# Block-sparse attention into a hard-swish MLP: k, q and x turned by the DMA crossbar instead of TensorE and VectorE

## The chip, the cores and the metric

The kernel runs on one core of one Trainium2 chip. The metric is the time of one execution in microseconds (us); the times shown are those of three executions, and one more execution was recorded by the hardware profiler. Engines are called PE (TensorE), ScalarE (ACT), VectorE (DVE), POOL (GpSimd) and SP (SyncE, which here only issues DMAs).

## The reference

q, k and v have 4 batches, 8 heads, 768 rows and 64 columns in float32. Each row attends to its neighbours at a distance below 16 and to 24 block summaries (the maximum of k and the mean of v over blocks of 32 rows). The output of all heads, 3072 x 512, goes through two matrix products with a hard-swish between them.

```python
k_sum = k.reshape(B, H, nb, block, D).max(axis=3)
v_sum = v.reshape(B, H, nb, block, D).mean(axis=3)
scores_l = scale * np.matmul(q, k.transpose(0, 1, 3, 2))
mask_l = np.abs(pos[:, None] - pos[None, :]) < window
scores_s = scale * np.einsum('bhsd,bhnd->bhsn', q, k_sum)
scores_s = scores_s + np.log(block)
scores_l_m = np.where(mask_l, scores_l, -1000000000.0)
scores_all = np.concatenate([scores_l_m, scores_s], axis=-1)
...
v_all = np.concatenate([v, v_sum], axis=2)
...
x = np.ascontiguousarray(attn_out.transpose(0, 2, 1, 3)).reshape(B * S, H * D)
...
h = x @ w_in
relu6 = np.clip(h + 3.0, 0.0, 6.0)
g = h * relu6 / 6.0
return (g @ w_out).astype(np.float32)
```

## The kernel before

Queries are handled in 12 tiles of 64 per batch and head. A tile t sees 96 keys: 32 rows ahead of its own window start, then 64 rows, and 24 block summaries, 120 in all. `kaug[p]` holds them for head pair p with the head columns on the partitions: [128, 12 tiles, 128], columns 0 to 31 the rows ahead, 32 to 95 the tile's own rows, 96 to 119 the block maxima. `vaug[i]` (two buffers, batch b uses b % 2) holds v with keys on the partitions, rows 0 to 31 being the rows ahead, 96 to 119 the block sums. q is shifted by 16 rows against k and lies turned in `qT`. Half 0 of a batch is tiles 6 to 11, half 1 tiles 0 to 5.

The steps, by the tags that they carry in the order text (tag, batch, index):

- **K, Q, V, I, O, Q01w**: loads by POOL, with a cast to bf16: k, q, v, w_in in four parts, w_out in four parts, and the rows of q for batch 0's half 1 (`qwide`). Batch 0's k and q come in their own layout (`knat`, `qnat`). Batch 1 comes in rows (`load_nat`, `nat`), batches 2 and 3 in blocks of 32 columns (`load_raw`, 32x96x32 pieces, `kraw` and `qraw`).
- **k0p, q0p**: batch 0's k and q turned by PE transposes, copied out of PSUM; `q_rest` (q0p1) turns q of half 1 from `qwide` on PE.
- **w1p** (`turn_nat`): per head pair, six PE transposes of k and six of q, copies out of PSUM, the copy of the rows ahead (`third`) and the block maxima (`maxima`). **w2p, w3p** (`turn`): the same for batches 2 and 3, but k and q turned by VectorE in 32x32 blocks.
- **h0cx**: the rows ahead of v in batch 0, copied by ScalarE or VectorE (`halo`); **H1 to H3** (`halos`): the same for batches 1 to 3 by two DMAs within SBUF, issued by SP.
- **u** (`vsum`): block sums of v on PE, then copies into `vaug`.
- **s** (`scores`): 12 small matmuls per half, exponential on ScalarE, mask on VectorE. **v** (`values`, `finish`): values, normalisation into `xn`, and xn turned into `x`: by PE and a copy for batches 0 and 1, by a crossbar DMA on SP (line 745) for batches 2 and 3.
- **F** (`f1`): first MLP product of a tile of 384 tokens (line 771), r on ScalarE (776), g on VectorE (778). **G** (`f2`): second product (791), copy, store by SP (802, 803). Eight token tiles s = 2 * batch + half.

What runs in which order on each engine is written out by hand: the `ORDER` text lists every step as tag.number, with :A or :D for the engine where ScalarE and VectorE are both possible. A small planner (`Plan.run`) walks the text, gives out the PSUM banks and buffers, and reckons a start for each step from costs that stand in the code; the program is issued in the order of these starts, and each engine takes its own instructions in that order. `keep` puts idle matmuls on PE into gaps that the planner reckons ahead of 23 us. Line 479 is the helper by which all copies go, line 876 the idle matmuls. SP and POOL also take their DMAs in order, and at most eight DMAs are open on each side (a ninth waits for the first).

Of the kernel before, what the change touches and what calls it, by code (L numbers as in the profile page):

```python
# [29 lines left out]
K01.0 K02.0 c.0 z2.0 z0.0 e.2 e.3 c.8 z3.0 z1.0 Q000.0 K00.0 c.2 Q010.0 c.4 e.1 V00.0 c.1 k02.0 k01.0 k02.1 e.0 s030.0 k03.0  # L30
k02.3:A k03.2:A q010.0 k02.2:A q010.1:A q000.0 q000.1:A q020.0 k01.1 k03.1 k03.3:D k03.4 k00.0 q030.0 q030.1:A s030.1 s030.2
V01.0 V02.0 V03.0 c.6 Q01w1.0 Q01w0.0 I0.0 Q01w2.0 c.7 k00.1 k00.3:D q020.1:D h010.0:A k01.4 s010.0 u00.0 u00.1:A k01.2:A
h000.0:A u01.0 s000.0 s010.1 h011.0:D k00.2:D k00.4 u02.0 s000.1 k01.3:D s010.2 u00.2:A s000.2 u03.0 h020.0:D u01.1:D u01.2:D
h030.0:D u01.3:D k02.4 s020.0 s020.1 u02.1:A s020.2 u03.1:A v00.0 c.9 v01.0 v01.2 u00.3:D v00.1 v02.0 v00.4 v00.2 v01.3 v00.3
v02.2 v00.5 v01.1 v01.4 u03.2:D v02.1 v00.6 v00.7:A h021.0:A I1.0 Q10.0 I3.0 K13.0 Q11.0 I2.0 c.3 K14.0 K12.0 K10.0 K15.0
K11.0 v01.5 v02.3 q021.0 q001.0 v01.6 v02.4 v02.5 q001.1:D v02.6 v01.7:D u02.2:D q031.0 v02.7:A h031.0:A q031.1:A F00.10
F00.11 F00.0 F00.1 F00.2 F00.3 q021.1:D F00.15 F00.12 q011.0 F00.16 Q14.0 Q13.0 c.5 q011.1:D F00.4 F00.17 Q12.0 Q15.0 V11.0
s001.0 s001.1 F00.13 s011.0 F01.0 s011.1 F01.1 F00.5 F00.6 F00.7 F00.14 s001.2 F01.2 h001.0:D V13.0 V12.0 V10.0 s021.0 s021.1
F01.9 F00.8 F01.10 s021.2 F00.9 F01.11 F01.6 s031.0 s031.1 F03.0 F03.6 F01.7 F03.1 s011.2 s031.2 F03.7 v03.0 v04.0 F01.8
F03.2 v03.1 F03.8 v04.1 v03.2 v04.2 F03.3 F02.3 F03.4 F02.4 F02.6 v05.0 v03.3 F02.7 v03.4:A F03.5 v05.1 v05.2 F02.5 F03.9  # L40
F03.10 v05.3 v04.3 F02.8 F03.11 v05.4:A v04.4:D O0.0 O1.0 O2.0 F02.9 w10.0 w12.0 F02.10 w12.1:A F10.0 F10.1 w10.1:D F02.11
F01.3 F01.4 F10.2 F01.5 w10.3 w13.0 w11.0 F12.9 F12.10 F12.11 w13.1:A F12.6 w10.4:D w11.1:D F13.3 F12.7 F12.8 F13.4 F13.5
w13.5 F13.9 F13.10 F12.3 F02.0 F02.1 F13.11 w13.6:D F02.2 F12.0 w12.5 w11.5 w12.6:D F12.4 w10.2:A F12.5 w12.2:D F12.1 F12.2
F11.0 w10.5 F11.3 w11.6:A F11.1 F11.4 F10.6 F10.7 w10.6:D s100.0 s100.1 s100.3 F11.2 w12.3 w12.4:D F11.6 G00.0 s120.0 F10.8
w11.3 F11.5 F11.7 w13.3 w11.2:D F11.8 w13.4:D O3.0 G00.1 F13.0 F10.3 s120.3 w13.2:A s120.1 F13.1 s130.0 s130.1 s130.3 F10.4
G00.2 F13.2 s130.2 s100.2 s120.2 s100.4 F10.9 F13.6 F10.10 w11.4:A G00.3 G00.4:A H1.0 H1.1 u1.0 u1.1:A F13.7 u1.2:A u1.4:A
G01.0 s110.0 G01.1 G01.2 G01.3 s110.3 s110.1 u1.8:D F13.8 s130.4 u1.6:D F10.5 s110.2 s120.4 s110.4 F10.11 F11.9 v10.0 v10.1
v10.2 u1.3:A G01.4:A v10.5 v10.6 V21.0 K20.0 K21.0 V20.0 K22.0 K23.0 V23.0 Q20.0 Q23.0 V22.0 Q21.0 K30.0 K31.0 Q22.0 G02.0
v10.3 G02.1 v12.0 v10.4:D v12.1 v12.2 u1.9:D u1.5:A F11.10 v10.7 G02.2 v12.3 G02.3 v10.8:A F11.11 w21.0 w20.0 w23.0 v12.4:A
u1.7:A F22.9 F20.0 G02.4:A F20.1 v13.0 F22.10 F20.2 v13.5 F22.11 F20.6 F20.7 F20.8 v13.6 F21.3 F21.4 v13.1 v13.2 w23.2:D  # L50
F21.5 G10.0 F22.0 F22.1 F22.2 G10.1 F20.3 F20.4 F20.5 v13.3 F20.9 F23.9 F20.10 v13.4:A F23.10 w22.0 F20.11 w22.2:D F22.3
F22.4 F23.11 v15.0 u2.0 u2.1:D w23.3 F22.5 F22.6 F21.6 G10.2 w20.2:A F21.7 F22.7 v15.1 w20.1 F21.8 F22.8 w20.5:D F21.0 F21.1
F21.2 v15.2 G10.3 G01.5 G10.4:A H2.0 G10.5 K32.0 Q33.0 K33.0 Q32.0 V30.0 V31.0 Q31.0 V32.0 V33.0 Q30.0 F23.6 F23.7 w23.1
F21.9 F21.10 v15.3 v13.7 v13.8:A F23.3 G21.0 u2.6:D F23.8 w23.4:D F23.4 F23.5 w23.5:A v15.4:A F23.0 u2.4:D u2.2:D F21.11
u2.5:D w20.3 F31.9 s230.0 F23.1 s230.3 s230.1 F31.10 F30.3 F23.2 w21.1 w22.1 G21.1 F30.4 w20.4:D F30.0 F30.1 u2.9:A u2.3:A
G21.2 F30.2 F30.5 w21.2:D G21.3 w21.3 F31.11 G21.4:A s200.0 u2.8:A F32.0 F32.1 F32.2 w30.0 w22.5:A s200.3 G12.0 F30.9 F33.0
G12.1 G12.2 G12.3 F33.1 w21.5:A s200.1 F30.10 s200.4 s230.2 w22.3 w21.4:D s210.0 F30.11 w30.3 w31.0 s230.4 w22.4:D F33.2
s210.1 G02.5 G00.5 G12.4:A G21.5 G12.5 F33.6 F33.9 u3.0 H2.1 s210.3 F33.7 F33.10 u3.1:A G11.0 s220.0 F31.3 F33.8 u3.2:D
u2.7:A F31.4 w31.3 u3.7:D s200.2 F33.11 F31.5 s220.1 s220.3 s220.2 s210.2 s220.4 w30.1 s210.4 w30.5:D F33.3 G11.1 G11.2 G11.3
F32.3 w33.1 F32.4 F32.5 w33.5:D F30.6 v23.0 G11.4:A F30.7 G20.0 G20.1 G20.2 G20.3 u3.3:A F33.4 w31.4:A G20.4:A F30.8 v23.1  # L60
u3.5:D v23.2 u3.6:D v23.4 v23.5 F33.5 w31.1 F32.6 F31.6 F31.7 F32.9 w30.2:A F32.7 F32.10 v25.0 v22.0 v25.1 v25.2 v22.1 F32.11
v22.2 G22.0 G22.1 F31.0 G22.2 G22.3 F31.1 w32.1 F32.8 w33.0 v23.3 v23.6 H3.0 F31.8 F31.2 G20.5 v25.3 G22.4:A F53.9 v20.0
v20.1 v20.4 v20.2 F50.0 F50.1 F50.2 F53.10 F50.6 G30.0 F50.7 F50.8 F53.11 F53.6 F50.9 G30.1 G30.2 F51.9 G30.3 w32.0 w32.2:D
F53.7 F53.8 w33.3 w33.4:D u3.9:D F51.10 F50.10 F51.11 G30.4:D F50.11 F52.0 F52.3 G32.0 F52.6 F52.1 w33.2:A F52.7 v20.5 F52.2
F52.8 G32.1 v20.3 v20.6 G11.5 G22.5 H3.1 v22.3 G30.5 s330.0 F51.3 F53.0 G32.2 F51.4 s330.1 F52.4 F53.1 s330.3 F51.5 F51.6
# [157 lines left out]
def kernel(  # L223
# [699 lines left out]
```

## Time and profile before

| | |
|---|---|
| three executions | 231.6, 233.06, 233.15 us (median 233.06) |
| the profiled execution: its own time | 232.96 us |
| its span in the trace | 231.3 us |
| PE busy | 219.8 us (95%), 2183 matmuls |
| VectorE busy | 157.4 us (68%), 350 instructions |
| ScalarE busy | 122.1 us (53%), 241 instructions |
| POOL busy | 63.3 us (27%), ended by 93 us |
| DMA packets | 115,914, mean 100 GB/s |

The span counts from the first to the last instruction recorded; the execution's own time has 1.66 us around it. Matmuls overlap, so a busy PE is not a full PE: the spacing between the starts of two matmuls says what they cost. Two lines of the profile by which it is read further: an idle time is shown ahead of the instruction that waited, with what ended it, and a DMA has a time to landing, from its issue to the moment at which its data can be used.

### The profile page before, as it was taken

What the parts mean: (1) busy time and instruction counts of PE and PEld (TensorE: products, weight loads), DVE (VectorE), ACT (ScalarE), POOL (GpSimd) and SP (SyncE); (2) the same over time, 40 slices, a digit from 0 to 9 for tenths busy, and PEclk for the clock granted to TensorE, in tenths of its full rate; (3) what the DMA queues carried; (4) which work ended last, traced back from release to release, by engine and by line L of the source; (5) the groups of instructions that cost most, each with busy time, mean ns of one, the idle gap of its engine ahead of it and who ended that gap; (6) DMA issues with size and microseconds to landing.
All of it is one profiled execution on the core that took longest, in us unless ns stands there. A gap on an engine that the chain in (4) does not pass through costs nothing.

```text
span 231.3 us, 5341 instructions
## 1 busy us (share of the span) xinstructions
PE 219.8 (95%) x2183; PEld 121.7 (53%) x2183; DVE 157.4 (68%) x350; ACT 122.1 (53%) x241; POOL 63.3 (27%) x76
## 2 busy tenths in 40 slices
PE   7999898999989999999999799999999999999993
PEld 2456475666544555555554455554655455555552
DVE  6378679979847989989998494795773344334210
ACT  2069197669966655797554235955334424254201
POOL 7998679542475719000000000000000000000000
PEclk9999999999999999999999999999999999999999
DMA  5999999999999999991016205102214201101142
GB/s 79 178 163 190 189 169 154 185 214 157 127 123 127 139 103 112 189 160 50 4 26 137 47 0 147 43 0 94 47 26 97 98 10 48 45 0 45 46 138 92
DMA packets 115914, 23.11 MB, mean 100 GB/s; under 512 B 107057, under 2 KB 112945, under 8 KB 115889
## 3 DMA queue, kind: packets, MB, share of 16 engines
q0 software_dynamic: 95712, 13.64, 100.5%
q1 hardware_dynamic: 20176, 9.13, 16.5%
q8 instruction: 17, 0.28, 0.5%
q14 instruction: 9, 0.07, 0.1%
HBM read 27.26 MB, written 6.29 MB: 145 GB/s over the span
## 4 chain that ended last, share of the span: by engine, by line
PE 60%; DMA 21%; POOL 7%; DVE 6%; ACT 2%; issue 1%; DVEq 0%; SPq 0%; ACTq 0%; POOLq 0%
PE h L771 26%; PE o L791 25%; DMA vaug<-vaug 9%; DMA win<-in_moe_w_in_dram 8%; PE h L791 5%; DMA vaug<-in_v_dram 3%; POOL vaug L431 3%; PE S L698 2%; DVE g L778 2%; PE S L570 1%; DMA x<-xn 1%; DVE kaug L625 1%; PE S L610 1%; POOL first L378 1%; DVE xn L735 1%
## 5 line engine op out<-in xcount | busy, mean ns | idle before, releaser
L771 PE MATMUL h<-x,win 128*128 128x384 bf16 (+1 forms) x536 | 95.4, 319 | 3.2 <-DMA x<-xn 1.7
L778 DVE SCALAR_TENSOR_TENSOR g<-r,h 128x384 bf16<-128x384 f32 x128 | 67.3, 546 | 34.8 <-ACT r L776 33.9
L776 ACT ACTIVATE r<-h 128x384 f32<-128x384 f32 x128 | 60.2, 493 | 56.5 <-PE h L771 53.2
L791 PE MATMUL o<-wout,g 128*128 128x512 bf16 x336 | 81.9, 379 | 0.0
L771 PEld LDWEIGHTS <-win 128*128 128x128 bf16 x536 | 49.2, 98 | 38.1 <-issue 4.0
L791 PEld LDWEIGHTS <-g 128*128 128x128 bf16 x400 | 38.3, 98 | 37.4 <-DVE g L778 0.4
L579 ACT ACTIVATE at<-S 120x768 bf16<-120x768 f32 x32 | 25.3, 811 | 4.8 <-PE S L570 4.3
L431 POOL DMA_DIRECT2D vaug<-in_v_dram x16 | 15.1, 945 | 11.9 <-PE S L698 4.9
L479 ACT COPY ot<-o 128x512 f32<-128x512 f32 x16 | 9.4, 588 | 14.8 <-PE o L791 14.8
L583 DVE TENSOR_TENSOR at<-at,mask 96x768 bf16<-96x768 bf16 x28 | 14.5, 545 | 3.8 <-ACT at L579 3.6
L735 DVE TENSOR_TENSOR xn<-S,rc 128x512 bf16<-128x512 f32 (+1 forms) x25 | 15.6, 639 | 0.5 <-DVE rc L731 0.2
L876 PE MATMUL o<-idle 128*128 128x512 bf16 x37 | 12.5, 476 | 1.6 <-DVE idle L305 1.5
L667 DVE TENSOR_REDUCE red<-kaug 128x24 bf16<-128x768 bf16 x12 | 11.4, 946 | 0.0
L570 PEld LDWEIGHTS <-kaug 64*128 64x128 bf16 x384 | 6.9, 95 | 7.5 <-issue 2.3
L791 PE MATMUL h<-wout,g 128*128 128x256 bf16 (+1 forms) x64 | 10.6, 326 | 0.0
L731 DVE RECIPROCAL rc<-S 128x8 f32<-128x8 f32 (+1 forms) x25 | 4.6, 193 | 8.3 <-PE S L698 8.2
L570 PE MATMUL S<-qT,kaug 64*128 64x64 bf16 x384 | 9.1, 191 | 0.9 <-DVE kaug L524 0.7
L698 PEld LDWEIGHTS <-at 120*64 120x64 bf16 x360 | 7.0, 111 | 5.1 <-issue 5.0
L876 PEld LDWEIGHTS <-idle 128*128 128x128 bf16 x51 | 5.3, 112 | 8.2 <-issue 3.8
L698 PE MATMUL S<-vaug,at 120*64 120x65 bf16 x352 | 8.6, 197 | 0.2 <-issue 0.2
L479 ACT COPY vaug<-vs 24x768 bf16<-24x768 bf16 x10 | 8.3, 828 | 0.2
L479 ACT COPY kaug<-h 128x576 bf16<-128x576 bf16 (+3 forms) x6 | 2.5, 495 | 9.5 <-DVE red L515 9.4
(109 smaller groups left out, 170.9 us busy)
## 6 DMA issues: line engine op xcount, KB each, us to landing
out_dram<-ot SPq DMA_DIRECT2D x19, 256.0 KB, 2.3
vaug<-in_v_dram POOLq DMA_DIRECT2D x16, 192.0 KB, 7.5
win<-in_moe_w_in_dram POOLq DMA_DIRECT2D x4, 512.0 KB, 9.0
wout<-in_moe_w_out_dram POOLq DMA_DIRECT2D x4, 512.0 KB, 12.1
first<-in_k_dram POOLq DMA_DIRECT2D x6, 192.0 KB, 16.0
first<-in_q_dram POOLq DMA_DIRECT2D x6, 192.0 KB, 8.9
vaug<-vaug SPq DMA_DIRECT2D x3, 380.0 KB, 8.5
out_dram<-ot SPq DMA_DIRECT2D x4, 224.0 KB, 2.3
```

What stands on the lines that cost most here:

```text
L431: op("POOL", 0.945, lambda: nc.gpsimd.dma_start(out=o[BLK:WIN, lo:hi, 0:D], in_=rows[:, lo:hi]), w=[("v", b % 2, c)], dma=1.28, els=1536)
L479: {"ACT": nc.scalar.copy, "DVE": nc.vector.tensor_copy, "POOL": nc.gpsimd.tensor_copy}[eng](o, i)
L570: nc.tensor.matmul(X[p, half].slot[:, j, i * QB:(i + 1) * QB], kaug[p][rows, t], qT[rows, p, t * QB:(t + 1) * QB], start=not masked, stop= ...
L579: op("ACT", 0.81, lambda a=a, x=x: nc.scalar.activation(a, x.slot[0:KEYS, :, 0:HALF], AF.Exp, scale=scl), r=[x], w=[("at", p, half)])
L583: op("DVE", 0.55, lambda m=m, half=half: nc.vector.tensor_tensor(m, m, mask[:, low(half):low(half) + HQ].unsqueeze(1).to_broadcast([WIN, 2 ...
L698: nc.tensor.matmul(y, a[:, cols], vaug[b % 2][0:KEYS, h, t, 0:D + 1], start=True, stop=True)
L735: nc.vector.tensor_tensor(o, src[..., 0:D], r.unsqueeze(len(r.shape)).to_broadcast(list(o.shape)), op=ALU.mult)
L771: nc.tensor.matmul(h.slot[:, lo * 128:hi * 128], w_in_sb[:, kt, ft * 128:(ft + 1) * 128], xt[s].slot[:, kt, lo * 128:hi * 128], start=(kt ...
L776: op("ACT", 0.49, lambda: nc.scalar.activation(r.slot[:], h.slot[:, 0:HALF], AF.Relu, bias=0.5, scale=1.0 / 6.0), r=[h], w=[r], alloc=r)
L778: op("DVE", 0.553, lambda: nc.vector.scalar_tensor_tensor(gt[s].slot[:, ft], r.slot[:], 1.0, h.slot[:, 0:HALF], op0=ALU.min, op1=ALU.mult) ...
L791: nc.tensor.matmul(o.slot[:, a:z], gt[s].slot[:, ft, ts * 128:(ts + 1) * 128], w_out_sb[:, ft, a:z], start=(ft == 0), stop=(ft == NFT - 1))
L876: nc.tensor.matmul(o, idle[:, 0:128], idle[:], start=True, stop=True)
```

## The change

- Batches 1, 2 and 3 are loaded alike, in rows (`load_nat(b, ...)`, 128x8x64 pieces), into two buffers `nat[b % 2]`; `load_raw` goes.
- k is turned by SP with crossbar DMAs, one for each tile of 64 rows and all four head pairs (`k_turn`, tags k1t to k3t, 12 per batch), straight into `kall`, the one tensor of which the four `kaug` are now parts. q is turned in the same way, one DMA for 128 rows (`q_turn`, tags q0w to q3w, 6 per batch and 3 for batch 0's half 1), into `qT`, now one tensor for each half. The PE transposes of `q_rest` and `turn_nat` and VectorE's block transposes go, with their copies.
- x of batch 1 is turned by SP's crossbar DMA, as x of batches 2 and 3 was.
- The rows ahead of v are copied by ScalarE or VectorE in all batches (`halo`); the two DMAs of `halos` go. `third` and `maxima` stay.
- The rule for idle matmuls is another, and with the planner's starts 19 of them are issued instead of 51: 9 instead of 25 ahead of the first transposes.
- `ORDER` is new throughout. Among what it moves: two of the half 1 scores of batch 0 ahead of the first F; w_in behind three more loads; w_out ahead of v of batch 1; a load of v of batch 3 ahead of the last loads of v of batch 2.

The counts of instructions: PE loses 48 + 12 + 24 transposes (of k and q of batch 1, q of batch 0, x of batch 1); VectorE loses 16 block transposes; SP's crossbar DMAs go from 12 to 75, its copies within SBUF from 6 to 0; POOL has 73 instructions instead of 60 in its list.

```diff
-    kaug = [sb([128, NQ, 128], BF16, f"kaug{p}") for p in range(NP)]
-    qT = sb([128, NP, PAD + S], BF16, "qT")
-    first = sb([128, 2 * NP * NB, BLK], BF16, "first")
...
+    kall = sb([128, NP, NQ, 128], BF16, "kall")
+    kaug = [kall[:, p] for p in range(NP)]
+    qT = [sb([128, NP, HALF], BF16, f"qT{x}") for x in range(2)]
+    both = [sb([128, 2 * NS, d_model], BF16, f"nat{i}") for i in range(2)]
+    nat = [{n: t[:, i * NS:(i + 1) * NS] for i, n in enumerate("KQ")} for t in both]
...
+        either = {"ACT": 0.83 + 0.08 * x, "DVE": (0.38 if b else 0.55) + 0.1 * x}
+        op(EITHER, either, go, r=[("v", i, c)] + ([] if b else [("vz", 0, c)]), w=[("vh", i, c, x)], free=[("sum", i)] if b > 1 else ())
-
-    def halos(b):
...
-    def q_rest(p):
...
+    def q_turn(b, u):
+        plan.at(f"q{b}w{u}")
+        src = nat[b % 2]["Q"] if b else qwide
+        n = NS // 2
+        to = qT[int(u < n)]
+
+        def go():
+            nc.sync.dma_start(out=to[:, :, u % n * 128:(u % n + 1) * 128], in_=src[:, u], transpose=True)
...
+    def k_turn(b, t):
+        plan.at(f"k{b}t{t}")
+        rows = slice(64 * (t % 2), 64 * (t % 2) + 64)
+
+        def go():
+            nc.sync.dma_start(out=kall[:, :, t, BLK:WIN], in_=nat[b % 2]["K"][rows, t // 2], transpose=True)
...
     def turn(b, p):
 
         plan.at(f"w{b}{p}")
-        red, w = Buf("red"), kaug[p]
-        op("DVE", 0.96, lambda: nc.vector.transpose(
...
         third(p)
-        maxima(p, red)
...
+        maxima(p, Buf("red"))
...
-        if b > 1:
+        if b:
             op("SP", 1.3, lambda: nc.sync.dma_start(out=xt[s].slot[:, :, cols], in_=xn.slot[:], transpose=True),
                r=[xn] + done, dma=0.6, kind="turn", **new)
             return
...
-            if o.begin < SLOW:
-                n = int((o.begin - end) / 0.43 + 0.1 + (not first and any(d.dma for d in o.deps)))
-            else:
-                n = max(int((o.begin - end) / 0.216), int(o.begin > last + 0.8))
+            n = int(max(min(o.begin, SLOW) - end, 0.0) / 0.43 + max(o.begin - 0.25 - max(end, SLOW), 0.0) / 0.216)
```

The new order on SP, from its list: the three turns of `qwide`; batch 1's 18 turns of k and q; three k turns of batch 2, x of batch 1 and stores, the remaining turns of batch 2 mixed with them; then the same with batch 3 and x of batch 2; then x of batch 3 and stores.

More of the change, by code (lines that the diff above doesn't have):

```diff
@@ L399, in load_wide, with load_nat @@
         op("POOL", 0.89 + 0.5 * (u == 0), go, w=[("qw", u)], dma=0.88, els=1024)
[L401 to L413 removed]
+    def load_nat(b, name, u):
+        plan.at(f"{name}{b}{u}")
         src, shift = (k, 0) if name == "K" else (q, PAD)
@@ L556, in scores @@
         masked = b == 0 and parts[0][1] == 0
-        p = parts[0][0]
+        p, half = parts[0]
         if masked:
@@ L663, in go @@
             copy(eng, w[:, 0, 0:BLK], w[:, NQ - 1, QB:WIN])
-        op(EITHER, {"ACT": 0.61, "DVE": 0.33}, go, r=[("ka", p, 0), ("ka", p, 1)], w=[("kh", p)])
+        op(EITHER, {"ACT": 0.61, "DVE": 0.33}, go, r=[("kt", t) for t in range(NQ)], w=[("kh", p)])
     def maxima(p, red):
@@ L668, in maxima @@
             red.slot[:], kaug[p][:, :, BLK:WIN].rearrange("p t (n c) -> p t n c", n=2), axis=AX.X, op=ALU.max),
-           r=[("ka", p, 0), ("ka", p, 1)], w=[red], alloc=red)
+           r=[("kt", t) for t in range(NQ)], w=[red], alloc=red)
         op(EITHER, {"ACT": 0.43, "DVE": 0.235}, lambda eng: copy(
@@ L747, in finish @@
             return
-        Y = Buf(("o", "h") if b == 0 and half == 0 else "S")
+        Y = Buf(("o", "h") if half == 0 else "S")
         def tr():
@@ L832 @@
         values(0, (T,), banks=banks, by_pair=True)
+    for u in range(NS // 2):
+        q_turn(0, u)
     for p in range(NP):
-        q_rest(p)
         scores(0, [(p, 1)])
@@ L839 @@
     for b in range(1, B):
-        if b == 1:
-            for name in "KQ":
-                for u in range(NS):
-                    load_nat(name, u)
-        else:
-            load_raw(b)
+        for name in "KQ":
+            for u in range(NS):
+                load_nat(b, name, u)
         for c in range(NP):
             load_v(b, c)
+        for t in range(NQ):
+            k_turn(b, t)
+        for u in range(NS):
+            q_turn(b, u)
         for p in range(NP):
-            turn_nat(p) if b == 1 else turn(b, p)
+            turn(b, p)
             scores(b, [(p, 0), (p, 1)])
+        if b > 1:
+            vsum(b)
+        for c in range(NP):
+            for x in range(2):
+                halo(b, c, x)
         if b == 1:
-            halos(b)
-        vsum(b)
-        if b > 1:
-            halos(b)
+            vsum(b)
         for Ts in ((0, 1), (2,), (3, 4), (5,)):
```

203 lines of the change are left out of this document (77 added, 126 removed).

## The prediction

> **What bounds the kernel now.** I read the busy shares first (PE 95%), then PE's timeline, because a share says nothing about which stage is full. Columns: start, length, engine, line, instruction, count; in brackets the idle time before it and what ended it.
>
> ```profile
> 1.52 8.50 PE L876 MATMUL o<-idle 128*128 128x512 bf16 x25 [1.52 <-DVE idle L305]
> 9.96 0.87 PE L494 MATMUL h<-ident,first 96*64 96x96 bf16 x32
> ...
> 30.61 2.15 PE L771 MATMUL h<-x,win 128*128 128x128 bf16 x28
> ...
> 47.06 0.83 PE L646 MATMUL S<-ident,kraw 128*128 128x128 bf16 x12
> 47.73 2.11 PE L771 MATMUL h<-x,win 128*128 128x384 bf16 x12
> ...
> 55.88 0.52 PE L570 MATMUL S<-qT,kaug 64*128 64x64 bf16 x24
> ...
> 65.32 0.85 PE L610 MATMUL S<-vaug,ind 96*32 96x128 bf16 x48 [0.87 <-DMA vaug<-vaug]
> ...
> 76.76 1.46 PE L771 MATMUL h<-x,win 128*128 128x384 bf16 x8
> ```
> ```profile
> 100.12 0.52 PE L570 MATMUL S<-qT,kaug 64*128 64x64 bf16 x24
> 100.57 0.82 PE L771 MATMUL h<-x,win 128*128 128x384 bf16 x4
> ...
> 128.50 0.81 PE L771 MATMUL h<-x,win 128*128 128x384 bf16 x4 [1.72 <-DMA x<-xn]
> ...
> 171.97 2.11 PE L771 MATMUL h<-x,win 128*128 128x384 bf16 x12
> 173.92 1.03 PE L791 MATMUL o<-wout,g 128*128 128x512 bf16 x4
> 174.79 0.81 PE L771 MATMUL h<-x,win 128*128 128x384 bf16 x4
> ...
> 216.95 10.56 PE L791 MATMUL h<-wout,g 128*128 128x256 bf16 x64
> ```
>
> The distance between two starts is what work costs PE: 4 first-layer matmuls 0.65 us (171.97 to 173.92 is 12), 4 second-layer 0.87, 24 scores 0.45, 12 transposes of 128x128 0.67 (47.06 to 47.73), hence 0.056 each. Multiplying PE's list after the first MLP matmul by such spacings gives 84.1 (first layer) + 83.3 (second) + 7.1 (scores) + 7.1 (values) + 2.5 (block sums) + 5.0 (transposes) = 189.0 us. PE starts the MLP at 30.6 and ends at 227.5, so 196.9 - 189.0 = 7.9 us are stalls. The last copy and store take 3.8. So 231.3 = 30.6 + 189.0 + 7.9 + 3.8. Laying the list beside the trace, the stalls have grown to 2.5 us at 55.9 (batch 1's first scores), 3.6 at 65.3, 4.3 at 76.8, 5.4 at 115, 7.5 at 128.5, and hardly after. The kernel is a start of 30 us, then PE without a gap to speak of.
>
> The chain of waits shows DMA at 21%, mostly weights, v and batch 1's 32 rows ahead (8.9% in vaug<-vaug): a chain that PE mostly covers with MLP work; only 0.87 us of it shows at 65.3.
>
> **What is removed.** PE: 12 transposes of q_rest, 48 of turn_nat, 24 of x of batch 1: 84 x 0.056 = 4.7 us. Nine of q_rest's lie before 30.6 (0.5), but 24 scores of batch 0's second half (0.5) now come ahead of the MLP, so the dense part falls from 189.0 to 184.3 and the start gets no PE work less. VectorE:
>
> ```profile
> L667 DVE TENSOR_REDUCE red<-kaug 128x24 bf16<-128x768 bf16 x12 | 11.4, 946 | 0.0
> ...
> L629 DVE STREAM_TRANSPOSE qT<-qraw 128x768 bf16<-128x768 bf16 x4 | 3.9, 969 | 0.0
> ```
> Sixteen stream transposes (15.2 us) and the PSUM copies of k and q (3.8) go, with 0.6 of edge copies; 14 more copies of the rows ahead (7 x 0.45, 7 x 0.62 with their second part) and a few copies taken over from ScalarE (2.5) come: -9.6 us on VectorE, about nothing on ScalarE (10 row-ahead pairs at 0.9 against 6 copies of x at 0.59, q and k copies 2.9 and others). VectorE ends none of the large PE gaps, so I count this at 0; if DVE-bound stalls hide in the 7.9, at most the 1.5 us that the waits put on g (1.2 and 0.3).
>
> **What is added.** SyncE had 12 crossbar turns; now 75: 36 of k (64x512), 21 of q, 18 of x.
>
> ```profile
> L745 SPq DMA_TRANSPOSE x<-xn x12: 1189/1236/1310, 118.9 to 177.8; - x12
> ...
> DMA to landing us min/median/max: 2.4/2.5/2.8
> ```
> A q turn has x's shape: 1.24 us of SyncE. A k turn is not in the trace. Below: half the bytes, half the time, 0.62. Above: the same, 1.24. I take 0.80: a plain store's 0.39 as the fixed part, half of the other 0.85 on it. All landings shown are on idle DMA engines; the new turns for batches 1 and 2 run beside loads. The nearest row is the row-ahead DMA, beside loads and later nearly alone:
>
> ```profile
> vaug<-vaug SPq DMA_DIRECT2D x1, 380.0 KB, 14.8
> ```
> ```profile
> vaug<-vaug SPq DMA_DIRECT2D x1, 380.0 KB, 5.4
> ```
> That is 2.7 times: a landing of 2.5 to 6.9; I take 4.7.
>
> The Trainium skill ("DMA: Bandwidth & Descriptors", Latency and other measured facts) gives a crossbar transpose 261 GB/s. An estimate from that page: 0.5 us for 128 KB, 0.25 for a k turn, so batch 1's queue below would take 5 us and never be waited for, and stalls would fall towards 6, a time near 226. The trace disagrees where it can: 128 KB in 1.24 us of issue is 106 GB/s.
>
> **On the path, batch 1.** kall is one buffer: a k turn waits for the last reader of its column block, batch 0's scores. The new list has the last of these 3.1 us of PE work after the first MLP matmul; with the usual lateness there, at 34.5. Behind k1t4 stand 10 k turns and 5 q turns on the same queue (11 x 0.80 + 5 x 1.24 = 15.0), loads being in by 40 as before. The last turn is issued at 48.3, lands at 53.0; maximum 0.95, copy 0.23, third 0.41 on VectorE: scores can start at 54.6. PE reaches them after 51.7 - 30.6 us of list plus the 2.5 us of stalls: 54.2. Stall 0.4. (k turns at 1.24 and 6.9: 61.6, stall 7; at 0.62 and 2.5: none.)
> Then VectorE has 13 us of maxima, copies, masks, row-ahead copies and g queued before the block sums can run (its list, by its rows): 66.0 against PE at 65.5. w_out is now loaded ahead of v of batch 1, which landed at 44.5 and will at some 52 to 54; the row-ahead copies come behind the maxima anyway, and the DMA pair that took from 44.5 to 65.2 is gone, so this moves nothing. Values 69.0 against 68.5. x of batch 1 then goes by SyncE: xn of the third tile at 73, landing 4.7: 77.8 against PE at 76.9 (75.6 to 80). Stalls by then about 4.9, where before has 4.3.
>
> **Batches 2 and 3.** SyncE serves in order, so turns of batch 2 stand behind those of x. From 74: 9 k (7.2), 7 q or x (8.7), 4 stores (1.6): 91.7, landing by 95; PE wants scores at 88.2 + 4.9 = 93.1. Stall 1.7. x of batch 2's first half, T 1 and 2 of batch 1's tile likewise, arrive within 1 us of PE. Batch 3: k turns from 105, the queue through at 127, landed 130, PE there at 132: nothing. The loads of K and Q of batches 2 and 3 fall from 16 x 3072 pieces to 24 x 1024, so the DMA engines are free earlier; POOL waits on nothing new but V3 ahead of V2, which has 30 us. I add 1.4 for lateness of that kind. Total stalls 8.0 against 7.9.
>
> **The start.** The run of idle matmuls before the first transposes falls from 25 to 9. In before the k transposes start at 9.96, right behind these, though the second k load (issued by 2.1, landing 4.8) was there at about 7; now they can start up to 2.5 us earlier. But VectorE's list from its first maximum to the copy of x grows from 17.9 to 20.3 us by rows (memsets, mask and halos moved in): +2.4. Sum 0; I keep 30.6, bounds 28 and 33. w_in is issued some 4 us later (18), landing about 24, still early enough.
>
> **Sum.** 30.6 + 184.3 + 8.0 + 3.8 = 226.7, against 231.3. The profiled execution took 232.96, 1.66 above its span and 0.1 below the median 233.06. So 226.7 + 1.8 = 228.5 us. A measurement here tells about 1% from no change: 2.3 us.
>
> **Rivals.**
> *A, slower: SyncE becomes the bound.* If a k turn costs what a q turn does, each batch's 12 add 5.3 us to a queue with 0 to 2 us of slack: batch 1 scores 4.8 late, batch 2 about 4, batch 3 some 2 to 4. 228.5 + 11.5 = 240. From about 1.0 us a k turn on (0.18 more x 26 turns on the path) it costs more than the 4.6 gained. For: 4 column blocks in both shapes. Against: half the rows.
> *B, slower: landings beside loads.* At 6.9 to 10 us instead of 4.7: 2 to 5 late for batch 1's scores, as much for its x; 234 to 237. For: 14.8 against 5.4. Against: fewer load pieces.
> *C, slower: a cold start.* In the first row an idle matmul lasts 634 ns until 7.0 us and 379 after: PE speeds up only after 5.5 us of unbroken work. Nine end at 5.4. If PE stays at half rate through the start, its some 10 us of transposes, scores, sums and values there double on a chain of latencies, perhaps 5 of it seen, and 2 at the MLP's start: 235. The Trainium skill ("TensorE: Matmul & The Clock Gate", Part 1: The HAM clock gate) says just this: the clock opens after a busy window of about 3.4 us. The trace agrees on the step, and no run here shows when a broken run opens it.
> *D, nothing gained:* the stalls take back what PE saves, as VectorE and SyncE chains set batch 1 and 2: 231 to 235.
> *E, faster still:* the start gains its 2.5 us, and 2 us of stalls go: 224.
>
> **Chances.** Forecast (226 to 230.5) 0.40, E 0.14, D around no change 0.14 (a little of it slower), A 0.14, B 0.12, C 0.06. Faster by over 1%: 0.54; within: 0.12; slower: 0.34. The range reaches to A: 223 to 240; the forecast's own is 225 to 231.
>
> **What would show it.** Right: no L646 group; PE dense from about 30; turns of k near 0.80 of SyncE; batch 1's scores near 55, block sums near 66, F on its x near 78, no stall over 2 us after 100. Wrong: k turns at 1.2, a wait of PE's scores on DMA kall or qT of several us, landings over 7 us, or idle matmuls and transposes at the slow pitch after 10 us.

## The result, and the profile after

The changed kernel takes 268.24 us (median of 4 runs, 265.1 to 269.77), the kernel before 233.11 us in the same comparison: a ratio of 1.143, 95% interval 1.133 to 1.153. Ratios are taken from fast runs alone (here 265.1 and 266.79 us, without the slow 269.68 and 269.77), while the times given are medians of all runs, and only the trace of the second buffer below is that of a slow run. Forecast were 228.5 us. The profiled execution has a span of 265.1 us against 231.3, 33.8 us more.

PE's timeline of the changed kernel, at the places that were shown of the kernel before:

```profile
31.34 0.82 PE L561 MATMUL S<-qT,kall 64*128 64x64 bf16 x24 [3.77 <-DMA qT<-qwide]
32.50 0.63 PE L732 MATMUL h<-x,win 128*128 128x128 bf16 x4
...
70.79 0.82 PE L561 MATMUL S<-qT,kall 64*128 64x64 bf16 x24 [15.09 <-DVE kall L463]
...
83.97 0.85 PE L602 MATMUL S<-vaug,ind 96*32 96x128 bf16 x48
...
100.70 4.00 PE L732 MATMUL h<-x,win 128*128 128x384 bf16 x12 [5.73 <-DMA x<-xn]
...
122.67 0.23 PE L561 MATMUL S<-qT,kall 64*128 64x64 bf16 x4
...
159.09 4.00 PE L732 MATMUL h<-x,win 128*128 128x384 bf16 x12 [7.13 <-DVE g L739]
```

No transposes of batch 1's k and q are left (the group of line 646). The page counts 2067 weight loads on PE, one for each matmul, instead of 2183: the 84 transposes and 32 idle matmuls are gone. (It counts 2042 matmuls, as some records are missing.) But how far PE lies behind the kernel before grows from step to step: 1.9 us at the first MLP matmul (32.50 against 30.61), 14.9 at batch 1's first scores (70.79, 55.88), 18.7 at its block sums (83.97, 65.32), 23.9 at the first layer on its x (100.70, 76.76), 27.3 at batch 2's first scores (122.67; the line of before stands below), 33.8 at the end. The 12 matmuls at 100.70 and at 159.09 take 4.00 us where before takes 2.11: PE's granted clock is 0.50 in the stretches 100 to 104 and 159 to 163.

```profile
95.39 0.52 PE L570 MATMUL S<-qT,kaug 64*128 64x64 bf16 x24
```

Rows of the page, before first, then after: 40 slices of the span, so 5.8 us each before and 6.6 after. DMA is the mean busy share of the 16 DMA engines in tenths (9 is 90% or more), PEclk the granted clock of PE, which before has a 9 in every slice.

```profile
DMA  5999999999999999991016205102214201101142
```
```profile
PEclk9999589995579995979999965999999999999999
DMA  5999999999999299999214355310021331003103
```

This is the view that the prediction left out. Already before, the DMA engines were busy for nine tenths or more in 17 slices one after the other, to about 104 us. Next to nothing waited for those loads (0.87 us at 65.32), so they hardly showed as a wait; the change put 35 short transfers, the turns that SyncE issues before 104 us, into the same stretch, and for these PE does wait.

What the turns cost, from the instructions of their line (duration on the queue in ns, least, median, most; then the time to landing in us), for k over the whole run and then between 36 and 70 us. EVENT_SEMAPHORE is a wait that stands ahead of a turn as an instruction of its own:

```profile
L540 SPq DMA_TRANSPOSE kall<-nat x36: 1170/1240/4164, 23.5 to 155.1; - x36
...
DMA to landing us min/median/max: 2.3/6.4/11.7
...
L540 SPq EVENT_SEMAPHORE  x6: 17/17/28, 38.7 to 59.4; - x6
...
DMA to landing us min/median/max: 6.3/7.5/11.7
```

And SyncE's queue for batch 1 (start, length, engine, line, operation, count):

```profile
36.84 1.79 SPq L531 DMA_TRANSPOSE qT<-nat  x1
38.80 5.08 SPq L540 DMA_TRANSPOSE kall<-nat  x4
43.98 1.22 SPq L531 DMA_TRANSPOSE qT<-nat  x1
45.24 1.25 SPq L540 DMA_TRANSPOSE kall<-nat  x1
46.58 4.40 SPq L531 DMA_TRANSPOSE qT<-nat  x2
51.08 5.49 SPq L540 DMA_TRANSPOSE kall<-nat  x2
...
58.07 5.28 SPq L540 DMA_TRANSPOSE kall<-nat  x4
```

The two at 51.08 take 5.49 us, one of them 4.16, and one of the two at 46.58 takes 3.08. The limit of eight open DMAs is not the reason: the waits ahead of the k turns take 17 to 28 ns here, and the DMA eight places before the longest issue, the k turn of 38.80, had landed at 45.07. The long issue ends at 55.24, just when the q turn of 43.98 lands (55.15); but the turn at 59.47 takes 1.26 us with six turns open. What makes an issue long stays open. On POOL the limit does hold loads up: the load of q at 36.14 starts when the one issued eight places before it, at 21.59, has landed (35.86), and batch 1's last load of k comes behind it, at 36.98.

VectorE shows how the wait spreads to work that needs no k:

```profile
157.63 0.95 DVE L628 TENSOR_REDUCE red<-kall 128x24 bf16<-128x768 bf16 x1 [7.70 <-DMA kall<-nat]
158.50 1.47 DVE L739 SCALAR_TENSOR_TENSOR g<-r,h 128x384 bf16<-128x384 f32 x3
```

PE's 7.13 us at 159.09 are put down to g, but g stood behind the block maximum of batch 3, which waited for k's last turn; batch 3's scores were wanted only at 172.

### The profile page after: what moved, and what is told of

Its sections match the earlier page's. It is cut to its first block, busy times and chain, and to the rows that moved or that the text cites. A ratio compares the mean times of both kernels' runs of the same rounds, so it can differ in the third digit from the quotient of the medians.

```text
span 265.1 us, 5198 instructions
## 1 busy us (share of the span) xinstructions
PE 218.8 (83%) x2042; PEld 120.7 (46%) x2067; DVE 150.5 (57%) x353; ACT 120.4 (45%) x232; POOL 64.0 (24%) x86
## 4 chain that ended last, share of the span: by engine, by line
PE 51%; DMA 24%; SPq 11%; POOL 7%; issue 3%; DVE 3%; ACT 1%; DVEq 0%; POOLq 0%
PE o L752 22%; PE h L732 21%; SPq L540 7%; DMA win<-in_moe_w_in_dram 6%; DMA kall<-nat 6%; DMA wout<-in_moe_w_out_dram 5%; PE h L752 4%; DMA vaug<-in_v_dram 3%; DMA qwide<-in_q_dram 3%; DMA x<-xn 2%; PE S L561 2%; SPq L531 2%; POOL vaug L425 2%; PE S L659 2%; POOL nat L414 1%
## 5 line engine op out<-in xcount | busy, mean ns | idle before, releaser
L732 PE MATMUL h<-x,win 128*128 128x384 bf16 (+1 forms) x536 | 101.5, 333 | 15.9 <-DVE g L739 9.6
L732 PEld LDWEIGHTS <-win 128*128 128x128 bf16 x536 | 52.1, 102 | 56.9 <-issue 23.2
L561 PE MATMUL S<-qT,kall 64*128 64x64 bf16 x384 | 9.9, 198 | 21.0 <-DVE kall L463 16.4
L628 DVE TENSOR_REDUCE red<-kall 128x24 bf16<-128x768 bf16 x12 | 11.3, 946 | 23.0 <-DMA kall<-nat 23.0
L561 PEld LDWEIGHTS <-kall 64*128 64x128 bf16 x384 | 7.5, 100 | 27.5 <-DVE kall L463 17.0
L414 POOL DMA_DIRECT2D nat<-in_q_dram x18 | 16.0, 890 | 14.7 <-DMA nat<-in_q_dram 5.5
L414 POOL DMA_DIRECT2D nat<-in_k_dram x18 | 16.1, 895 | 14.0 <-DMA vaug<-in_v_dram 4.9
L425 POOL DMA_DIRECT2D vaug<-in_v_dram x16 | 15.1, 955 | 14.5 <-PE S L659 13.6
L575 DVE TENSOR_TENSOR at<-at,mask 96x768 bf16<-96x768 bf16 x28 | 14.9, 550 | 2.0 <-ACT at L571 1.9
L463 ACT COPY vaug<-vaug 32x768 bf16<-32x768 bf16 (+2 forms) x21 | 12.1, 611 | 0.3
L463 ACT COPY kall<-kall 128x352 bf16<-128x352 bf16 (+1 forms) x6 | 1.8, 355 | 15.9 <-DMA kall<-nat 15.9
L841 PE MATMUL o<-idle 128*128 128x512 bf16 x13 | 5.6, 573 | 2.1 <-DVE idle L308 1.6
```

The costliest lines, as they stand in the source:

```text
L414: nc.gpsimd.dma_start(out=o[n:128], in_=src[b, :, lo + n:lo + 128].rearrange("h r d -> r h d"))
L425: op("POOL", 0.945, lambda: nc.gpsimd.dma_start(out=o[BLK:WIN, lo:hi, 0:D], in_=rows[:, lo:hi]), w=[("v", b % 2, c)], dma=1.28, els=1536)
L463: {"ACT": nc.scalar.copy, "DVE": nc.vector.tensor_copy, "POOL": nc.gpsimd.tensor_copy}[eng](o, i)
L561: nc.tensor.matmul(X[p, half].slot[:, j, i * QB:(i + 1) * QB], kaug[p][rows, t], qT[half][rows, p, i * QB:(i + 1) * QB], start=not masked, ...
L732: nc.tensor.matmul(h.slot[:, lo * 128:hi * 128], w_in_sb[:, kt, ft * 128:(ft + 1) * 128], xt[s].slot[:, kt, lo * 128:hi * 128], start=(kt ...
```

## The experiments

Ratios are against runs of the kernel before taken beside each experiment, with their 95% interval; the changed kernel is at 1.143. A point is one hundredth of that ratio. Where an experiment takes steps out or puts steps in, `ORDER` changes for these steps.

### Which part costs: taken out of the changed kernel

**k turns left out.**
```diff
-        for t in range(NQ):
-            k_turn(b, t)
```


> The changed kernel without the 36 k turns of batches 1 to 3 (their scores then read batch 0's k; all other work, order and bytes stay). Price theory (a k turn costs SyncE 1.24 us where 0.80 was counted, and the queue is served in order) and landing theory (turns take 7 to 12 us to land beside loads): both 228 to 238 us, batch 1's scores on PE at 52 to 56, no stall on k. Rival (the new order, the q turns, x of batch 1 or the row-ahead copies cost the time): 250 us or more, the 3.8 us at the start and the 5.7 us at x of batch 1 stay.

239.52 us, 1.028 (1.022 to 1.034), just above the range of both theories. The k turns are 11.5 of the 14.3 per cent. The rest of the change is no gain either: without them PE still waits 3.2 us for batch 0's q at 30, 3.2 for batch 1's q at 59, and 5.6 for v at batch 2's block sums. Of these only the first stood in an expectation.

**Batch 1's k and q on PE again.**
```diff
-            turn(b, p)
+            turn(b, p) if b > 1 else turn_nat(p)
```


> k and q of batch 1 are turned by PE again, as in the kernel before (48 transposes, 8 copies on ScalarE), the rest as changed. If batch 1's turns among the loads are the main loss: its wait of 15 us goes and the 2 us at half clock behind it, 2.7 us of PE work come back: 248 to 254 us, with the waits at x of batch 1 and at batch 3's turns as they are. If those later waits are only batch 1's lateness handed on: 235 to 242 us. If batch 1's turns are not the main loss: over 260.

259.06 us, 1.109 (1.101 to 1.118): 3.3 points, some 8 us, less than expected. Batch 1's first scores are back at 55.44, but the waits at x (6.24 us at 91) and in front of batch 3 (8.03 us at 152) stay or grow.

**x of batch 1 on PE again.**
```diff
-        if b:
+        if b > 1:
             op("SP", 1.3, lambda: nc.sync.dma_start(out=xt[s].slot[:, :, cols], in_=xn.slot[:], transpose=True),
```


> The changed kernel with x of batch 1 turned on PE again (24 transposes, copies on VectorE and ScalarE), the rest as changed. If the six x turns cost here what they cost in the kernel before (16 us, two waits of 7 us with the half clock behind them): 252 to 258 us. If the later waits close in behind it, because batch 3's turns start when batch 2's scores end and SyncE's queue sets that: 262 to 269 us.

264.75 us, 1.128 (1.115 to 1.142). The intervals of the two kernels overlap a little; at most a few us. The wait of 5.73 goes, the one in front of batch 3 is 8.13.

**A second buffer for kall and qT.**
```diff
-    kall = sb([128, NP, NQ, 128], BF16, "kall")
+    kall = [sb([128, NP, NQ, 128], BF16, f"kall{i}") for i in range(2)]
```


> kall and qT get a second buffer (batches take turns), so k and q turns need no longer wait for the scores of the batch before; the order on every queue stays. One-buffer theory (batch 3's turns start at 135 because batch 2's scores end there, and 20 us of SyncE work do not fit before PE wants them): the waits at 117 to 124 and at 159 go, batch 1's 15 us stays, 250 to 257 us. Landing theory (the DMA engines are full until 75 us, and that alone costs): 263 to 270 us.

(The kernel also has one buffer fewer for the copies of the block sums, `vs`, 3 instead of 4.) 1.097 (1.087 to 1.107), from runs of 255.29 and 255.98 us: 4.6 points. In the changed kernel SyncE's first k turn of batch 3 starts at 134.96, right after batch 2's last scores (134.66), and the last lands at 157.5; with the second buffer they start at 123, and in place of the 7.13 us PE waits 0.5. The waits at 116 to 124 didn't go, against the expectation: in this trace PE waits 4.97 us for g at 116. SyncE's queue stands from 80.4 to 87.9 before an x turn of batch 1 with nine k turns of batch 2 behind it, and from 93 on these land after 6 to 9 us, beside loads; no run tests whether that is the cause.

**The three together** (the last three edits in one kernel).


> The changed kernel with k, q and x of batch 1 on PE as before, and a second buffer of kall and qT, so that only batches 2 and 3 and batch 0's second q half are turned by the crossbar, in free time. If the loss is made by turns among the loads (batch 1) and by the one buffer (batches 2 and 3): 232 to 240 us. If SyncE's order and price alone delay batches 2 and 3 by more: 245 us or more, with waits on kall or qT after 110.

244.76 us, 1.043 (1.030 to 1.056), between the two ranges. The three parts alone gave 3.3, 1.4 and 4.6 points, 9.3 in all; together they give 10.0. So, within the intervals, these losses add up and don't hide each other. What is left lies at batch 0's q (3.0 us at 30), at ScalarE (1.4 and 1.7 us at batch 1's transposes, 2.4 at 104 for a copy of x) and at v of batch 2 (1.1 us).

### Price or landing

**Plain copies instead of k turns.**
```diff
-            nc.sync.dma_start(..., in_=nat[b % 2]["K"][rows, t // 2], transpose=True)
+            nc.sync.dma_start(..., in_=nat[b % 2]["K"][rows, t // 2].rearrange("r (j p c) -> r j p c", j=2, p=NP))
```


> Each k turn is replaced by a plain copy of the same 64 KB to the same place on the same queue, with the same waits (k is then not transposed). Price theory: a plain copy costs SyncE 0.4 to 0.7 us, so batch 1's last one is issued by 50 to 54 and the time is 232 to 242 us. Landing theory: as many bytes move beside the same loads, the landings stay at 6 to 10 us, and the time at 255 us or more.

262.83 us, 1.129 (1.124 to 1.134). A plain copy takes 0.60 us of the queue, half of a turn, and lands as late:

```profile
L540 SPq DMA_DIRECT2D kall<-nat x36: 590/600/2067, 23.4 to 154.7; - x36
DMA to landing us min/median/max: 2.2/6.5/12.4
...
74.44 0.90 PE L561 MATMUL S<-qT,kall 64*128 64x64 bf16 x24 [19.39 <-DVE kall L463]
```

Batch 1's scores come no earlier (74.44). While the loads run the price is not what binds batch 1.

**Half of the k turns from ScalarE.**
```diff
-            nc.sync.dma_start(out=kall[:, :, t, BLK:WIN], ...
+            (nc.scalar if t % 2 else nc.sync).dma_start(out=kall[:, :, t, BLK:WIN], ...
```


> The 18 k turns of the odd column blocks are issued by ScalarE, spread among its work, instead of SyncE. Price theory: SyncE's queue for batch 1 shrinks by 6 x 1.24 = 7.4 us, batch 1's scores come some 7 us earlier, as much is won over batches 2 and 3 together: 248 to 256 us. Landing theory: the DMA engines get the same packets in the same stretch: 262 to 270 us, turns issued earlier land as late.

304.29 us, 1.304 (1.294 to 1.314), far outside both. ScalarE stands still for 21.8 us:

```profile
63.36 1.29 ACTq L540 DMA_TRANSPOSE kall<-nat  x1
64.69 0.59 ACT L463 COPY x<-S 128x512 bf16<-128x512 bf16 x1 [21.78 <-issue]
```

Its first turn starts at 63.36. SyncE's last one of the batch was issued at 51.2 and landed after 12.0, at 63.2. The program itself makes ScalarE wait: four EVENT_SEMAPHORE instructions ahead of the turn wait for the eight semaphores of SyncE's DMAs, and the last ends at 63.3. The Trainium skill ("DMA: Bandwidth & Descriptors", DMA Transpose (X-bar)) says that two streams of transposes must not be under way at once, the later one having to wait until the earlier has landed in full; this program keeps to that, and no run here shows what happens without the wait. So this way of sharing the turns between two queues costs ScalarE the landing time of the other queue, and the run says nothing on price against landing.

**Later loads left out; w_out left out; both; both and plain copies.**
```diff
-        for c in range(NP):
+        for c in range(NP) if b == 1 else ():
             load_v(b, c)
...
-        op("POOL", 0.77, lambda: nc.gpsimd.dma_start(out=w_out_sb[:, c * w:(c + 1) * w], in_=...),
+        op("POOL", 0.77, lambda: nc.gpsimd.memset(w_out_sb[:, c * w:(c + 1) * w], 0.01),
```


> The loads of k, q and v of batches 2 and 3 are left out (their turns read batch 1's rows, their values batch 0's and 1's v). Landing theory: turns from 51 us on meet only w_out and v of batch 1, batch 1's late landings fall to 3 to 4 us, later ones to 2.5: 245 to 253 us. Price theory: SyncE's issue stays as it is, at most 3 us from the last landings of batch 1: 260 to 266 us.

> w_out is filled by memsets on GpSimd where its four loads were issued: 2 MB less for the DMA engines between 40 and 60 us, nothing else changed. Landing theory: v of batch 1 and the turns of batch 1 land some 10 us earlier (last k turn by 60 instead of 69), the wait of 15 us falls to 3 to 7 us, time 250 to 257 us. Price theory (16 turns of 1.24 us in order): the queue is hardly faster, the wait stays over 10 us, 261 us or more.

> Both leave-outs together: w_out is filled by memsets, and the loads of k, q and v of batches 2 and 3 are left out, so that nothing takes the place of w_out. From 47 us on batch 1's turns share the DMA engines with v of batch 1 alone. Landing theory: they land in 2.5 to 4 us, the queue runs at its issue price (39 + 16 x 1.24 = 59), last landing 62, batch 1's wait 15 falls to 6 to 9 us (in part as a wait on g): 250 to 257 us. Price theory alone: the wait stays at 12 or more, 260 us or more.

> As the run with both leave-outs, and each k turn a plain copy (k then not transposed). If price is what is left once landings are short: 12 x 0.6 = 7 us less of SyncE for each batch, batch 1's wait at 2 us or less, batch 3's gone, 240 to 248 us. If price never bound: within 3 us of the run without the plain copies.

Measured, with the place of batch 1's first scores in PE's timeline, and the time from there to the end of the span:

| | us | ratio | first scores | from there |
|---|---|---|---|---|
| before | 233.11 | | 55.9 | 175.4 |
| changed | 268.24 | 1.143 | 70.8 | 194.3 |
| plain copies | 262.83 | 1.129 | 74.4 | 188.2 |
| no later loads | 261.98 | 1.124 (1.117 to 1.131) | 71.9 | 187.2 |
| no w_out | 264.31 | 1.136 (1.127 to 1.145) | 68.1 | 197.3 |
| neither | 250.12 | 1.077 (1.070 to 1.083) | 60.1 | 188.0 |
| neither, plain copies | 238.73 | 1.025 (1.019 to 1.030) | 64.2 | 172.6 |

Without the later loads, and without w_out, the time is the one that the price theory gave. But without the later loads batch 1 is as late as ever, and by its landings (7.2 to 14.2 us for k between 36 and 75 us): w_out and v still fill the DMA engines; without w_out the later loads moved up into its place. Only with both gone does batch 1 come 10.7 us earlier. The landing theory holds for batch 1. After it the price counts, too: in that part 6.1 us with the loads there (194.3 to 188.2) and 15.4 us once they are gone (188.0 to 172.6), of which up to 4.1 us come from the flaw below; over the whole kernel it is 11.4 us (250.12 to 238.73, below the 240 expected). Landing and price are two limits of one queue: taking either away brings 6 to 7 us in the part behind the first scores, taking both away 17.6 to 21.7.

One flaw: the memsets on GpSimd, 7.06 us, held a copy of VectorE in two of these runs, no w_out and the last row (line 463, vaug from vf: 7.94 and 8.10 us instead of 0.3 to 0.7, ending 0.2 us after the last memset), and PE waited 7.4 and 8.0 us for g at 46 and 44. In the third run the copies were done before the memsets began. So in the last row the first scores are late (64.2 against 60.1) for a reason that the experiment brought in, and the turns behind them had that much more time; how much nearer to the kernel before that run would lie without it, it doesn't show.

### One part alone, added to the kernel before

**x of batch 1 by the crossbar.**
```diff
-        if b > 1:
+        if b:
```


> The kernel before with one part of the change alone: x of batch 1 goes by the crossbar on SyncE, which does little else there. PE saves 24 transposes, 1.3 us. If the six turns land in 2.5 to 5 us beside the loads of batches 2 and 3 they are hidden or nearly so: 231 to 234 us. If they land in 6 us or more, PE waits 3 to 5 us for x at 77: 235 to 238 us.

249.26 us, 1.070 (1.064 to 1.077), far above either. PE's timeline, and who waited for the x turns (us, times):

```profile
83.77 2.72 PE L771 MATMUL h<-x,win 128*128 128x384 bf16 x8 [7.17 <-DMA x<-xn]
109.24 1.44 PE L771 MATMUL h<-x,win 128*128 128x384 bf16 x4 [7.08 <-issue]
...
  PE h L771: 15.9, 3
```

SyncE's queue is all but empty here; six turns, beside the loads, cost 16 us. Of the wait at 109.24 PE's timeline names no releaser, but the view of the turns' line counts it to them, and the second x turn issued just before (101.43) landed at 109.15. In the changed kernel the same turns cost less, 1.4 points; that this is because PE is late there already is not shown.

**The rows ahead by engines.**
```diff
-        op("SP", 0.65, lambda: nc.sync.dma_start(out=o[0:BLK, 1:n, 0:D], in_=o[QB:WIN, 0:n - 1, 0:D]),
...
+        for c in range(NP):
+            for x in range(2):
+                halo(b, c, x)
```


> The kernel before with one part alone: the rows ahead of batches 1 to 3 are copied by VectorE and ScalarE (24 copies, some 10 us of engine time) instead of the two DMAs a batch. If this part is harmless: 230 to 235 us, the 0.9 us wait at batch 1's block sums gone. If VectorE's queue is the hidden bound: 236 to 242 us with new waits of PE on g.

236.47 us, 1.013 (1.009 to 1.017): slower, if little. The wait at the block sums goes, others on VectorE come (1.46 us on kaug at 62.7, 0.98 on g at 50.6). The rival was right, in kind and, just, in its range.

**Batch 0's second q half by the crossbar.**
```diff
-                nc.tensor.transpose(bank(T).bitcast(BF16)[:, u * 128:(u + 1) * 128], qwide[:, u, p * 128:(p + 1) * 128], ident[:])
+            nc.sync.dma_start(out=qT[:, :, u * 128:(u + 1) * 128], in_=qwide[:, u], transpose=True)
```


> The kernel before with one part alone: batch 0's second q half turned by three crossbar turns right behind its loads. PE saves 12 transposes and 3.4 us go from VectorE and ScalarE; the turns, issued at about 20 beside the loads of w_in, k and q, land in 8 to 10 us as in the changed kernel, so by 31: before's second-half scores start at about 46, so nothing waits: 230 to 234 us. If the three turns delay w_in or k and q behind them: 235 to 238 us.

237.77 us, 1.020 (1.006 to 1.034). The turns themselves cost nothing; the MLP begins at 29.84 instead of 30.61. But v of batch 1 is issued from 37.9 instead of 34, the row-ahead DMA at 48.09 instead of 44.50, and it lands later:

```profile
68.05 1.16 PE L610 MATMUL S<-vaug,ind 96*32 96x128 bf16 x48 [4.82 <-DMA vaug<-vaug]
```

The rival was right again. With three turns of 128 KB more for the DMA engines, w_in's last part lands at 35.92 instead of 31.73; POOL's load eight places behind it starts only then (36.20 instead of 32.01), and v of batch 1 stands behind that. Each of the three parts alone makes the kernel before slower.

### The clock, and the start

**Idle matmuls in three waits.**
```diff
+        if o.key in FILL:
+            todo.append(lambda n=FILL[o.key], s=...: keep(n, s))
```


> The changed kernel with idle matmuls inside its three long waits (64 ahead of batch 1's first scores, 22 ahead of the first layer on batch 1's x, 29 ahead of the one that waits for g at 159), fewer than each wait holds. If the half clock behind each wait costs 2 us of PE's own time: 261 to 265 us and full clock from 70 on. If PE's slower work is hidden by what comes late anyway: 266 to 270 us.

266.4 us, 1.142 (1.134 to 1.150): no change that can be told. (The last 29 write over a bank of batch 2's values that VectorE had yet to read, so the output is another.) The fillers did keep the clock up: 0.968 over the run instead of 0.916, and the 12 matmuls at 159.79 took 2.11 us. But batch 1's scores came at 72.86, 3.18 us after the last filler, and a wait of 6.12 us stood at 117 where 2.46 had been:

```profile
72.86 0.52 PE L561 MATMUL S<-qT,kall 64*128 64x64 bf16 x24 [3.18 <-DVE kall L463]
...
117.38 1.44 PE L732 MATMUL h<-x,win 128*128 128x384 bf16 x4 [6.12 <-DVE g L739]
```

Three waits filled, some 2 us of PE's own work each, gave nothing that can be told: what PE wins it waits for at the next late transfer.

**The old rule for idle matmuls.**
```diff
-            n = int(max(min(o.begin, SLOW) - end, 0.0) / 0.43 + max(o.begin - 0.25 - max(end, SLOW), 0.0) / 0.216)
+            if o.begin < SLOW:
+                n = int((o.begin - end) / 0.43 + 0.1 + (not first and any(d.dma for d in o.deps)))
+            else:
+                n = max(int((o.begin - end) / 0.216), int(o.begin > last + 0.8))
```


> The changed kernel with the rule of the kernel before for idle matmuls at the start (40 instead of 19). If the cold clock until 17 us costs the start: the MLP begins by 30 instead of 32.5 and the time is 264 to 266 us. If the q turns of batch 0's second half (landed at 31.3) set the MLP's start: no change, 267 to 270 us.

267.92 us, 1.150 (1.143 to 1.156). The MLP begins at 31.83 instead of 32.50, and nothing is won. The cold start is not the cause.

### The change in a better form

**Six wide k turns a batch, into a tile of their own.**
```diff
+            nc.sync.dma_start(out=kT[:, :, u * 128:(u + 1) * 128], in_=nat[b % 2]["K"][:, u], transpose=True)
```


> The changed kernel with k turned by 6 turns of 128x512 a batch, into a tile of its own, instead of 12 of 64x512; 12 more copies on ScalarE put it in place. The same bytes are turned. If a turn is paid by the piece (1.24 us for either shape) and the wait for the scores of the batch before is what else delays them: SyncE's k work halves to 7.4 us a batch, turns of batches 2 and 3 start as soon as k is there, 248 to 256 us, the wait at 159 gone. If only the bytes beside the loads count: 262 us or more.

258.4 us, 1.109 (1.103 to 1.116), between the two ranges.

```profile
L539 SPq DMA_TRANSPOSE kT<-nat x18: 1189/1248/5142, 22.3 to 136.8; - x18
DMA to landing us min/median/max: 2.4/6.9/14.1
...
71.60 0.82 PE L561 MATMUL S<-qT,kall 64*128 64x64 bf16 x24 [11.70 <-DVE kall L463]
```

Twice the bytes at the same price (1248 against 1240 ns): a turn is paid by the piece. Batch 1's scores come at 71.60 all the same, and the bytes that move beside the loads are as many as before; the gain of some 8 us lies behind them, where the wait at 159 is gone. This run doesn't separate fewer pieces from the tile of its own, which also does what the second buffer does.

**The same, with x of batch 1 on PE** (this edit and the third of the first group).


> As the run with wide turns, and x of batch 1 on PE again. If with the queue relieved x of batch 1 shows its price (two waits and the half clock): 4 to 8 us less than the run with wide turns alone. If its waits are taken over by batch 2's turns: within 3 us of it. Either way not below 235 us, since batch 1's wait among the loads stays.

252.71 us, 1.083 (1.076 to 1.091): 5 to 6 us less, as expected once the queue has room. No form that was tried beats the kernel before.

## Why the prediction was wrong

- **What bounds the kernel.** PE without a gap was right, and the matmuls taken off it went. The term that failed is the stalls. In the prediction's own sum the changed kernel is 32.5 + 184.3 + 44.9 + 3.4 = 265.1 us: start, dense part and end nearly as forecast, the stalls 44.9 us where 8.0 were put (a remainder, so it holds PE's work at half clock, too). PE's timeline names 15.1 us of it at batch 1's scores, 9.6 for g and 6.2 for x. The step behind that term is the reading of DMA's 21% in the chain as "a chain that PE mostly covers": the DMA row of the same page, full to 104 us, was not read. In that stretch the turns landed after 6 to 14 us, on idle DMA engines after 2.3.
- **Landing, 4.7 us (2.5 to 6.9).** Measured 6.3 to 11.7 for k between 36 and 70 us, up to 13.7 for q: beyond the upper end. The row at hand, 14.8 us for a DMA within SBUF in the same stretch, was nearer than the 2.7 ratio made of it.
- **Loads "in by 40 as before".** The last k load of batch 1 was issued at 36.98 and landed 9.8 later, at 46.8; v of batch 1, forecast 52 to 54, needed 20 to 23 us from its issue at 44.5 to 47.3.
- **A k turn at 0.80 us.** It is 1.24, the upper bound; halving the bytes saves nothing. The estimate from the 261 GB/s of the Trainium skill ("DMA: Bandwidth & Descriptors", Latency and other measured facts), 0.25 us, is further off: 64 KB in 1.24 us of issue are 53 GB/s.
- **Batch 1's queue.** Forecast: k1t4 at 34.5, last turn issued at 48.3, landed 53.0, scores 54.6. Measured: 38.80, 63.45, 70.32, 70.79. Of the 16.2 us, 2.3 are batch 0's scores ending later (36.84), 2.0 a q turn that waited for the same scores and stood ahead of k1t4, 4.8 the price (11 turns of 0.44), 6.0 issues longer than that price (two of them 4.8) with the pauses between, 2.2 the last landing; 1.1 come off, as the last turn is one of q and needs no maximum behind it.
- **Batch 3, no wait.** "k turns from 105" forgot the step's own rule that kall is one buffer: they can't start before batch 2's last scores, which stand at 109.8 in the kernel before, too. Measured start 134.96, a wait of 7.13 us; the second buffer, 4.6 points, shows it.
- **VectorE counted at nothing.** Its list was shorter by 7 us (150.5 against 157.4) and that gained nothing, as said. That a maximum waiting for k holds up g behind it was not said, and PE waited 9.6 us for g, 7.1 of it shown at 159.
- **x of batch 1, row-ahead copies, q_rest,** each costed at nothing or a gain: 16, 3 and 5 us when added to the kernel before alone.
- **The start, 30.6.** 32.50, by the 3.77 us for batch 0's q turns (landing after 6 to 10 us beside loads).
- **Rivals.** The result lies beyond all of them. A had the premise right (1.24) and with 240 us only a part of the sum. B had the place right and the size wrong (6 to 14 us, not 6.9 to 10). They were taken as one or the other; they hold together, on the same queue, and the single buffer comes on top. C is refuted by the old idle rule. The rule of the Trainium skill that it names ("TensorE: Matmul & The Clock Gate", Part 1: The HAM clock gate) fits what the trace shows after the waits at 100.70 and 159.09 (4.00 us for 2.11), but filled waits show that this sets no time here. D and E, stalls as before or fewer, did not come about.

What stays open: how much of the last 2.5 points (loads, price gone) is the memset's doing, what makes single issues of SyncE long, and why the second buffer left the waits at 116 to 124.

## What to carry to other kernels

Before a transfer that something waits for is put into a stretch, read the DMA row there: where it stood at 9 here, a short transfer took 6 to 14 us to land instead of 2.3, and as only eight loads may be open on POOL, late landings held up the issue of the loads behind them. Work that costs PE 0.06 us a transpose, on an engine that stalls nowhere else, is cheap against that. For each buffer that a queue of turns writes, ask for every batch, and not just the first, when its last reader is done; and see what stands behind the instruction that waits for it, in order, on its engine.

## What the runs showed of the hardware that was not expected

- A crossbar turn of 64x512 and one of 128x512 both take 1.24 us of the issuing queue; a plain copy of the 64 KB takes 0.60. On idle DMA engines a turn lands after 2.3 us.
- Beside loads that keep the DMA engines busy, the same turns landed after 6 to 14 us, and a plain copy of 64 KB was no quicker (median 6.5 against 6.4 us over the run).
- A copy on VectorE that takes 0.3 to 0.7 us took 7.94 and 8.10 us while GpSimd ran four memsets in a row.
